# A delta rule and two expert layers on one core: one written order for all engines to the end of block 0, weights converted in pairs

## The chip, the core and the metric

One core of a Trainium2 chip runs one program. The metric is device time in microseconds, the median of repeated runs. The profile is one execution, taken by the hardware profiler.

## The reference, cut to what matters

```python
for t in range(S):                      # delta rule: B=4, H=8, S=768, D=48
    y[:, :, t] = einsum('bhd,bhde->bhe', q[:, :, t], state)
    v_old = einsum('bhde,bhd->bhe', state, k_n[:, :, t])
    state = state + beta_t * einsum('bhd,bhe->bhde', k_n[:, :, t], v[:, :, t] - v_old)
x = y as (3072, 384)
h = x @ w_in                            # layer 1: 384 -> 2048 -> 384
g = where(h >= 1, h, where(h <= -1, 0, (h + 1) ** 2 / 4));  x = g @ w_out
h = x @ w2_in;  r = maximum(h, 0);  out = (r * r) @ w2_out   # layer 2, same sizes
```

All inputs are float32; the kernel is handed the weights as the 64-bit words that the harness makes of them.

## The kernel before, in words

The sequence is cut into 24 chunks of 32 steps. For a chunk, small matmuls make the products of its keys (`gram`), a triangular matrix of 32 by 32 per batch and head is inverted (`tri`, for a group of up to four chunks at once, group sizes `GROUPS` = 2, 4, 4, ...), and then `chunk_steps` runs a chain: `ks` (state times keys, subtracted from the values on VectorE), `tr` (the inverse applied), `qs`/`pu` (the output), `ku` (the state's update), `xt` (transposition into `xh`, `xl`, the high and low parts that the expert layer multiplies). Chunks 0 and 1 (`HEADS`) have no state yet and use `cross_gram`.

The expert layers run in blocks of chunks (`SIZES` = 2, 2, 3, ...; block 0 is chunks 0 and 1, 256 columns). A block has 16 units f. Unit f multiplies `w_in` tile f (`hidden`: 9 matmuls into `h`), makes g on ScalarE and VectorE (L606 to L609), splits it into `gh` (ScalarE, L621) and `gl` (VectorE, L622), and two units later `out1` adds 9 matmuls into `acc`. Each block's third copy out of `acc`, like the converted tiles of layer 2, takes a buffer of the ring `wl`.

Each matmul operand is a high and a low part, so each weight tile must first be converted: ScalarE takes its two words apart (L178, L181, into tiles `wt` and `wl`), VectorE joins them (L187), ScalarE rounds to the high part (L198), VectorE subtracts for the low part (L202). A tile is 128x384; layer 1 has 32. `load_w` keeps at most two weight loads under way.

The order: to the end of the first inversion (on VectorE, in halves) everything stands as written. After that only TensorE's order is written (`manual_schedule(engines=ENGINES)`); a scheduler places the instructions of the other engines by its own estimates. The second group's inversion runs on GpSimd in 30 steps of a product (L423) and a sum (L424). Conversions are handed out by `more_w1`: 20 steps between the pieces of chunks 0 and 1, the rest in the slots of block 0 (two slots a unit). Block 0's slots from `HEAD` = 19 on also carry the steps of chunks 2 and 3, and slot 18 the transpose that ends the second inversion (`end1`, L427).

Of the kernel before, what the change touches and what calls it, by code (L numbers as in the profile page):

```python
# [25 lines left out]
def kernel(  # L26
# [39 lines left out]
    EAGER = 18  # L66
    AHEAD = 8
# [3 lines left out]
    WT, WL = 3, 4  # L71
    GB = 2
    MANY = 4
    HEAD = 19
# [14 lines left out]
    pairs = {}  # L89

    def weight(i, f):

        if (i, f) not in pairs:
            t = wp.tile([P, 2, DM], F32R, tag=f"w{i}{f}", name=f"w{i}{f}")
            pairs[i, f] = t[:, 0], t[:, 1]
        return pairs[i, f]
# [56 lines left out]

    def load_w(x, key):
        w, f, i = key
        pool, tag, bufs = ring, "raw", RAW
        if w == 0:
            pool, tag, bufs = wp, f"w{i}{f}", 1
        raw = raws[key] = pool.tile([P, DM, 2], I32, tag=tag, bufs=bufs, name="raw")
        ins = nc.sync.dma_start(  # L160
            raw.rearrange("p a b -> p (a b)"), (w1, w2)[w][f, i].bitcast(I32)
        ).ins
        if w == 0:
            sent.append(ins)
            if len(sent) > FLIGHT:
                tc.add_manual_dep(
                    ins, sent[-1 - FLIGHT].name,
                    mybir.DependencyInfo(mybir.DependencyClass.Sync, mybir.DependencyReason.DATA),
                    reason="at most FLIGHT weight loads under way",
                )  # L170


    def convert_stages(key, box):
        def s0():
            raw = raws.pop(key)
            t = box["w"] = tmp("wt", WT)
            b = box["t"] = tmp("wl", WL)
            nc.scalar.activation(  # L178
                t, raw[:, :, 1].bitcast(F32), AF.Prelu, scale=2.0 ** -112, alpha=2.0 ** 32
            )  # L180
            nc.scalar.activation(  # L181
                b.bitcast(I32), raw[:, :, 0].bitcast(U32), AF.Copy, scale=7.49 * 2.0 ** -32
            )

        def s1():
            t, bits = box["w"].bitcast(I32), box["t"].bitcast(I32)
            nc.vector.scalar_tensor_tensor(  # L187
                bits, t, 3, bits, ALU.logical_shift_left, ALU.bitwise_or
            )

        return [s0, s1]


    def part_stages(key, box):
        _, f, i = key

        def s3():
            nc.scalar.copy(weight(i, f)[0], box["t"])  # L198

        def s4():  # L200
            hi, lo = weight(i, f)
            nc.vector.tensor_sub(lo, box["t"], hi.bitcast(F32))  # L202

        return convert_stages(key, box) + [s3, s4]
# [3 lines left out]
    def weight_items(w):  # L208

        keys = [(w, f, i) for f in range(NF) for i in range(2)]  # L210
        if w == 0:
            keys.sort(key=lambda k: (k[1] + LAG * k[2], -k[2]))

        def item(x):
            _, f, i = keys[x]
            box = {}
            if w == 0:
                r = part_stages(keys[x], box)
            else:
                r = convert_stages(keys[x], box)  # L220
                r.append(lambda: nc.sync.dma_start(w2f[f, :, i], box["t"]))
            s1 = r[1]
            r[1] = lambda: (s1(), ahead(x + 1 + (RAW if w else AHEAD)))
            return r

# [3 lines left out]
        def ahead(end):  # L229
            while todo and todo[0][0] < end:  # L230
                load_w(*todo.pop(0))
# [34 lines left out]
    def value(c):  # L266

        g, j = group_of[c]
        nc.gpsimd.tensor_mul(
# [10 lines left out]
    def gram(c, lo=0, hi=2, late=0, eng=None, side=0):  # L280
# [43 lines left out]

    spare = {
        name: f"w{i}{NF - f}" for name, i, f in
        (("u0", 1, 1), ("u1", 1, 2), ("cross", 0, 1), ("z", 1, 3), ("l", 0, 2), ("d", 1, 4))
    }

    def cross_gram(a, c):  # L330
        x = cross[a, c] = wp.tile([P, H, 2, T], F32, tag=spare["cross"], name="cross")
# [14 lines left out]
    def tri(n, eng, halves=False):  # L346
        x = tx
        gm = ring.tile([P, T, T], F32, tag="gm", bufs=1, name="gm")
# [36 lines left out]
        def row():  # L385
            if halves:
                d = two(gm, both, both)
                eng.tensor_mul(
# [6 lines left out]
        def row2():  # L395
            if halves:
                eng.tensor_mul(
# [10 lines left out]
        def step(j):  # L408
# [15 lines left out]
            eng.tensor_add(rest, rest, t)  # L424
# [11 lines left out]
    def joined(n):  # L436
        l, z = (wp.tile([P, 2, H, T], F32, tag=spare[k], name=k) for k in "lz")
        d = wp.tile([P, GC * H, T2], F32, tag=spare["d"], name="d")
# [30 lines left out]
    def chunk_steps(c):  # L469
# [26 lines left out]
        def tr():  # L496
# [7 lines left out]
            else:  # L504
                us[c] = wp.tile([P, H, D], F32, tag=spare[f"u{c}"], name="u")
# [78 lines left out]
    def hidden(layer, n, f):  # L584
# [18 lines left out]
        if layer == 0:  # L603
# [3 lines left out]
            marks[1] = nc.vector.tensor_scalar(g, r, 2.0, 0.5, ALU.min, ALU.mult)  # L607
            nc.scalar.activation(g, g, AF.Square)  # L608
            nc.vector.scalar_tensor_tensor(g, r, -1.0, g, ALU.add, ALU.max)  # L609
        else:  # L610
# [3 lines left out]
        def rest():  # L614
# [6 lines left out]
            nc.scalar.copy(ghi, g)  # L621
            nc.vector.tensor_sub(glo, g, ghi.bitcast(F32))  # L622
            gs[layer, n, f] = (ghi, glo)
# [74 lines left out]
    def flow(items, lag=1):  # L698

        steps = []  # L700
        for x, it in enumerate(items):
            for i, st_ in enumerate(it):
                while len(steps) <= x * lag + i:
                    steps.append([])
                steps[x * lag + i].append(st_)
        return [lambda fs=fs: [f() for f in fs] for fs in steps]

# [7 lines left out]
    first1, w1s = weight_items(0)  # L715
    first2, w2s = weight_items(1)
    w1f = flow(w1s)
    w1f.reverse()

    SPREAD = 3  # L720
    behind = [nullcontext]

    def more_w1(m=1):
        with behind[0]():
            for _ in range(m):
                if w1f:
                    w1f.pop()()

    with tc.manual_schedule():
        for c in range(GROUPS[0]):  # L730
            load_kq(c)
        nc.sync.dma_start(bet, beta)
        for c in range(GROUPS[0], KQ):
# [3 lines left out]
        for c in range(HEADS):  # L737
            load_kv(c)
        first1(EAGER)
        nc.gpsimd.memset(zero, 0.0)  # L740
        nc.gpsimd.memset(one, 1.0)
        nc.gpsimd.memset(tiny, 1e-36)
        nc.scalar.activation(st[:, 0, 0, 0:1], one, AF.Sqrt, bias=zero)
        nc.gpsimd.memset(mask, 1.0)
        nc.gpsimd.memset(tx, 0.0)
        for b in range(B):
            for o, op in enumerate((ALU.is_ge, ALU.is_gt)):
                m_ = mask[T * b:T * (b + 1), o]
                nc.gpsimd.affine_select(
# [5 lines left out]
        for c in range(GROUPS[0]):  # L755
            gram(c, 0, 1)
        begin, pre, steps, end = tri(0, V, True)
        begin()
        go(pre)
        for c in range(HEADS):  # L760
            save0(c)
        go([gram(c, late=2, eng=G) for c in range(GFIRST[1], GFIRST[2])])
        cross_gram(0, 1)
        masks = [gram(c, 1, 2, late=2, eng=G) for c in range(HEADS)]
        go(steps)
        for c in range(HEADS):
            value(c)
        go(masks)
        end()
        rows0()  # L770
        begin, pre, steps, end1 = tri(1, G)
        begin()
        ins = go(pre[:-2])
        behind[0] = lambda: tc.issue_after(ins.ins)
    ENGINES = {mybir.EngineType.PE}
    with tc.manual_schedule(engines=ENGINES):
        for f in (ld0, dld0):
            for c in range(HEADS):
                f(c)
        go(pre[-2:])  # L780
        go(steps)
        chains = [chunk_steps(c) for c in range(HEADS)]
        (k0, t0, q0, p0, _, x0), (k1, t1_, q1, p1, _, x1) = chains
        for m, fs in enumerate([[k0, t0], [k1], [q0, p0], [t1_], [q1], [x0], [p1], [x1]]):
            go(fs)
            if m < 4:
                more_w1(5)
        behind[0] = lambda ins=marks[2]: tc.issue_after(ins.ins)
        turn[0] = None
        load_kv(HEADS)  # L790
        for c in range(KG):
            load_kg(KQ + KG + c)

        SL = 2 * NF
        exa, exb = {}, {}

        def put(n, slot, *fs):
            for i, f in enumerate(fs):
                exb.setdefault(SL * n + slot + i, []).append(f)

        def later(*fs):

            def one_(f):
                with tc.issue_after(marks[0].ins), tc.issue_after(marks[1].ins):
                    f()

            return [lambda f=f: one_(f) for f in fs]

        def put_a(n, slot, f):
            exa.setdefault(SL * n + slot, []).append(f)  # L810

        at, ready = {}, {}

        def two_grams(c):
            gram(c)
            gram(c + 1, side=1)

        after = {}
        for i, c in enumerate(range(GFIRST[2], GFIRST[3])):
            ready[c] = 4 + 3 * i
            put_a(0, ready[c], lambda c=c: gram(c))
        for g in range(3, NG):
            for i in range(GROUPS[g] // 2):
                after[GFIRST[g - 1] - 1 + i] = GFIRST[g] + 2 * i
        for n in range(1, NB):
            todo = []
            for c in range(FIRST[n], FIRST[n] + SIZES[n]):  # L830
                for i, s_ in enumerate(chunk_steps(c)):
                    todo.append(((at, c) if i == 0 else None, s_))
                if c in after:
                    x = after[c]
                    todo.append(((ready, x + 1), lambda x=x: two_grams(x)))
            for i, (mark, s_) in enumerate(todo):
                o = 0 if n > 1 else HEAD
                slot = SL * (n - 1) + o + i * (SL - o) // len(todo)
# [3 lines left out]
        put(0, HEAD - 1, *later(end1))  # L842
        for c in range(HEADS):
            put(0, 8 + 4 * c, lambda c=c: load_kq(c + KQ))
        for c in range(HEADS, NCH):
# [17 lines left out]
        for n in range(NB - 1):  # L863
            if n == 0:
# [95 lines left out]
```

## Time and profile before

| | us |
|---|---|
| median of 3 runs (1023.9 to 1025.18) | 1024.61 |
| the profiled execution | 1026.46 |
| its span, first to last instruction | 1024.7 |
| TensorE busy (95% of the span) | 968.4 |
| VectorE / ScalarE / GpSimd busy | 574.5 / 465.2 / 319.4 |

Engines are PE (TensorE), PEld (its weight loads), DVE (VectorE), ACT (ScalarE), POOL (GpSimd) and SP (which issues the DMAs). A row of a timeline names start, duration, engine, line, operation and tiles; in brackets stands how long the engine was idle before and what released it; "issue" means that it waited for nothing that the profile shows. A float32 matmul of the program shows as two rows' counts, a float32r one as one.

### The profile page before, as it was taken

To read this page: it belongs to the slowest core of one execution; us is meant where nothing else is said; L and a number is where in the kernel's file an instruction comes from. 1 tells how busy PE (TensorE), PEld (TensorE's weight loads), DVE (VectorE), ACT (ScalarE), POOL (GpSimd) and SP (SyncE) were. 2 spreads that over 40 slices of the span, in tenths; PEclk is the share of its full clock that TensorE was granted. 3 is DMA by queue.
4 is the path that set the end of the run, shared out by engine and by line. 5 is a ranking of instruction groups with operands and counts; after the bars stand their busy time and mean duration, and the time that the engine had idled before them with its cause. 6 is when DMAs were issued, how large, how long until landed. Compare 5 with 4: busy or idle time off the path is not lost.

```text
span 1024.7 us, 32087 instructions
## 1 busy us (share of the span) xinstructions
PE 968.4 (95%) x14152; PEld 902.6 (88%) x14152; DVE 574.5 (56%) x994; ACT 465.2 (45%) x935; POOL 319.4 (31%) x476
## 2 busy tenths in 40 slices
PE   5357899999999999999999999999999999999998
PEld 4347898999999999999999999989989999899997
DVE  6988565775666677677465676543343333333333
ACT  2776465554555545555445554333333333333332
POOL 3792780492077049368022121120020200200000
PEclk9999999999999999999999999999999999999999
DMA  9774154442532534312023223010010000000000
GB/s 265 222 215 142 49 152 133 129 142 61 174 101 80 157 88 133 111 39 96 3 71 90 67 79 95 6 55 8 1 62 1 1 32 1 31 1 1 31 1 31
DMA packets 35244, 80.83 MB, mean 79 GB/s; under 512 B 4512, under 2 KB 15264, under 8 KB 35104
## 3 DMA queue, kind: packets, MB, share of 16 engines
q1 hardware_dynamic: 35104, 78.78, 25.9%
q8 instruction: 111, 1.82, 0.8%
q14 instruction: 29, 0.24, 0.1%
HBM read 63.03 MB, written 15.73 MB: 77 GB/s over the span
## 4 chain that ended last, share of the span: by engine, by line
PE 87%; DMA 6%; DVE 3%; ACT 2%; issue 1%; SPq 0%; ACTq 0%; DVEq 0%
PE acc L574 39%; PE h L574 38%; DMA raw<-in_w_dram 5%; PE yy L518 2%; PE sps L530 2%; PE tr L498 2%; PE ks L484 2%; PE g L293 1%; PE yy L484 1%; PE xt L559 1%; DMA kqt<-in_kq_dram 1%; DVE wl L187 0%; DVE g L609 0%; DVE w L202 0%; DVE gp L427 0%
## 5 line engine op out<-in xcount | busy, mean ns | idle before, releaser
L574 PE MATMUL acc<-w,gg 128*128 128x384 f32 x1152 | 218.4, 337 | 2.1 <-ACT e L629 2.1
L574 PEld LDWEIGHTS acc<-w,gg 128*128 128x128 f32 x1152 | 204.5, 187 | 10.7 <-ACT e L629 3.0
L574 PE MATMUL h<-x2s,w 128*128 128x512 f32 x864 | 213.8, 392 | 0.0
L574 PEld LDWEIGHTS h<-x2s,w 128*128 128x128 f32 x864 | 160.9, 188 | 28.3
L574 PE MATMUL h<-xh,w 128*128 128x384 f32 (+1 forms) x864 | 164.6, 327 | 3.5 <-ACT r L606 2.8
L574 PE MATMUL acc<-gh,w 128*128 128x384 f32 (+1 forms) x864 | 163.7, 325 | 1.6 <-ACT gh L621 1.6
L612 DVE TENSOR_TENSOR rg<-rg 128x512 f32<-128x512 f32 x96 | 71.3, 743 | 141.4 <-ACT rg L611 141.4
L574 PEld LDWEIGHTS h<-xh,w 128*128 128x128 f32 x864 | 139.6, 193 | 6.7 <-ACT r L606 3.7
L574 PEld LDWEIGHTS acc<-gh,w 128*128 128x128 f32 x864 | 136.7, 189 | 5.2 <-ACT gh L621 1.7
L611 ACT ACTIVATE rg<-h,zero 128x512 f32<-128x512 f32 x96 | 66.0, 687 | 137.4 <-PE h L574 137.4
L622 DVE TENSOR_TENSOR gg<-rg,gg 128x512 fp32r<-128x512 f32 x96 | 66.7, 695 | 104.5 <-ACT gg L621 104.5
L622 DVE TENSOR_TENSOR gl<-g,gh 128x384 fp32r<-128x384 f32 (+1 forms) x144 | 88.0, 611 | 64.5 <-ACT gh L621 60.3
L423 POOL TENSOR_TENSOR t<-tx,gm 128x30 f32<-128x30 f32 (+9 forms) x180 | 110.0, 611 | 19.3 <-DVE tx L402 5.9
L621 ACT CAST gh<-g 128x384 fp32r<-128x384 f32 (+1 forms) x144 | 68.7, 477 | 102.7 <-DVE g L609 78.4
L606 ACT ACTIVATE r<-h,one 128x384 f32<-128x384 f32 (+1 forms) x144 | 78.3, 543 | 81.5 <-PE h L574 80.3
L424 POOL TENSOR_TENSOR tx<-tx,t 128x30 f32<-128x30 f32 (+9 forms) x180 | 110.6, 615 | 14.0
L621 ACT CAST gg<-rg 128x512 fp32r<-128x512 f32 x96 | 59.7, 622 | 119.7 <-PE acc L574 112.7
L609 DVE SCALAR_TENSOR_TENSOR g<-r,g 128x384 f32<-128x384 f32 (+1 forms) x144 | 88.5, 614 | 39.9 <-ACT g L608 37.4
L607 DVE TENSOR_SCALAR g<-r 128x384 f32<-128x384 f32 (+1 forms) x144 | 62.4, 434 | 68.1 <-ACT r L606 67.1
L608 ACT ACTIVATE g<-g 128x384 f32<-128x384 f32 (+1 forms) x144 | 70.2, 487 | 54.5 <-DVE g L607 53.7
L574 PE MATMUL acc<-gl,w 128*128 128x384 f32 (+1 forms) x432 | 90.8, 318 | 1.9 <-DVE gl L622 1.9
L574 PE MATMUL h<-xl,w 128*128 128x384 f32 (+1 forms) x432 | 91.8, 322 | 0.0
(99 smaller groups left out, 923.9 us busy)
## 6 DMA issues: line engine op xcount, KB each, us to landing
raw<-in_w_dram SPq DMA_DIRECT2D x64, 384.0 KB, 3.8
kqt<-in_kq_dram SPq DMA_DIRECT2D x88, 192.0 KB, 4.1
kv<-in_kv_dram SPq DMA_DIRECT2D x24, 384.0 KB, 3.6
w2f<-wl SPq DMA_DIRECT2D x32, 192.0 KB, 3.1
w2r<-w2f SPq DMA_DIRECT2D x16, 384.0 KB, 3.0
x2r<-x SPq DMA_DIRECT2D x6, 768.0 KB, 4.8
out_dram<-e SPq DMA_DIRECT2D x23, 192.0 KB, 2.0
x<-e SPq DMA_DIRECT2D x18, 192.0 KB, 2.1
```

Of the source, the lines that this page charges most:

```text
L423: eng.tensor_mul(t, by.to_broadcast(shape), of.to_broadcast(shape))
L424: eng.tensor_add(rest, rest, t)
L484: per_bh(lambda b, h, p, pd: nc.tensor.matmul(o[p, h], kqt[c][pd, b // 2, h, x * T:(x + 1) * T], st[pd, b // 2, h], start=h == 0, stop=x = ...
L574: nc.tensor.matmul(o, *((r, l) if swap else (l, r)), **flags)
L606: marks[0] = nc.scalar.activation(r, h, AF.Relu, bias=one)
L607: marks[1] = nc.vector.tensor_scalar(g, r, 2.0, 0.5, ALU.min, ALU.mult)
L608: nc.scalar.activation(g, g, AF.Square)
L609: nc.vector.scalar_tensor_tensor(g, r, -1.0, g, ALU.add, ALU.max)
L611: marks[0] = nc.scalar.activation(r, h, AF.Relu, bias=zero)
L612: marks[1] = nc.vector.tensor_mul(g, r, r)
L621: nc.scalar.copy(ghi, g)
L622: nc.vector.tensor_sub(glo, g, ghi.bitcast(F32))
```

## The change

Weights of layer 1 are loaded into tiles of two (`weights`), taken apart in place, joined, rounded and subtracted 768 wide; the layout of the spare rooms follows (`room`). `tri` gains an argument that no call uses. Both halves of the products of chunks 0 and 1 come from one set of matmuls (`gram_of_head`). The `wl` ring has three buffers instead of four, `wt` is gone. The first three loads of layer 2 move behind block 0, and the last six of layer 1 behind unit 3. Up to the end of block 0 the order of all engines is written; inside a unit the conversions stand at four fixed places (`between`). After it only TensorE's order is written, as before.

```diff
-    WT, WL = 3, 4
+    WL = 3
...
+    def sign_bits(raw):
+        low, high = raw[..., 0], raw[..., 1].bitcast(F32)
+        return (
+            lambda: nc.scalar.activation(high, high, AF.Prelu, scale=2.0 ** -112, alpha=2.0 ** 32),
+            lambda: nc.scalar.activation(
+                low, low.bitcast(U32), AF.Copy, scale=7.49 * 2.0 ** -32),
+        )
...
+    def upper(x):
+        nc.scalar.copy(weights(x)[:, :, 0], words[x])
+
+    def lower(x):
+        t = weights(x)
+        nc.vector.tensor_sub(t[:, :, 1], words.pop(x), t[:, :, 0].bitcast(F32))
...
+    EARLY, READY, HELD = 6, 3, 6
...
+        def part(x):
+            if x == 0:
+                if a is not None:
+                    make(a)
+                some(1)
+            elif x == 1:
+                if a is not None:
+                    upper(a)
+            elif x == 2:
+                some(1)
+            elif a is not None:
+                lower(a)
...
+        ins = go(steps)
+        rows0()
+        end()
+        after(value(0), ins)
+        value(1)
...
+        begin1()
+        s0()
+        t0()
+        pre1[0]()
+        whole_bits(2)
+        s1()
+        t1_()
+        go(pre1[1:])
+        steps1[0]()
+        value(2)
+        go(steps1[1:])
...
+        put_a(0, 4, k0)
+        put(0, 20, end1)
...
+        for c, at_ in ((2, (21, 22, 24, 26)), (3, (26, 27, 29, 31))):
...
-            a = max(a, HEAD) if g == 2 else a
+            a = max(a, 22)
...
+        for x in range(NF):
+            unit(x, between(x))
+    with tc.manual_schedule(engines={mybir.EngineType.PE}):
+        for x in range(NF, total):
+            unit(x)
```

ScalarE, from the copy of chunk 1's `u` (after `tr`) to its `xh`. Before:

```order
L506 COPY u<-tr 128x384
L181 ACTIVATE wl<-raw 128x384 x2
L198 CAST w_1084<-wl 128x384
L178 ACTIVATE wt<-raw 128x384
L181 ACTIVATE wl<-raw 128x384
L561 CAST xh<-xt 128x3x128
L198 CAST w_1094<-wl 128x384
L178 ACTIVATE wt<-raw 128x384
L198 CAST w_1212<-wl 128x384
L178 ACTIVATE wt<-raw 128x384
L181 ACTIVATE wl<-raw 128x384
L523 COPY kv<-yy 128x384
```

Changed (L549 is now the copy of `u`, L566 that of the output, L180 and L181 take a pair apart, L217 rounds it):

```order
L549 COPY room<-tr 128x384
L217 CAST w_852<-wl 128x2x384
L180 ACTIVATE raw<-raw 128x768
L181 ACTIVATE raw<-raw 128x768
L566 COPY kv<-yy 128x384 x2
L604 CAST xh<-xt 128x3x128
L217 CAST w_967<-wl 128x2x384
L604 CAST xh<-xt 128x3x128
```

Between the copy of `u` and that of the output stood ten conversion instructions before; now three, of two pairs.

VectorE around the transpose that ends the second inversion and the first subtraction of chunk 2's chain. Before (L427, L494):

```order
L393 TENSOR_TENSOR gm<-gm,st_1935 128x512
L607 TENSOR_SCALAR g<-r 128x256
L427 STREAM_TRANSPOSE gp<-tx 128x32x32
L622 TENSOR_TENSOR gl<-g,gh 128x256
L609 SCALAR_TENSOR_TENSOR g<-r,g 128x256
L494 TENSOR_TENSOR kv<-kv,ks 128x384
```

Changed (L468, L537), with a whole unit ahead of it: L650 and L653 make g, L187 joins a pair, L668 is `gl`, L221 subtracts the pair:

```order
L650 TENSOR_SCALAR g<-r 128x256
L187 SCALAR_TENSOR_TENSOR wl<-raw 128x768
L653 SCALAR_TENSOR_TENSOR g<-r,g 128x256
L668 TENSOR_TENSOR gl<-g,gh 128x256
L221 TENSOR_TENSOR w_1577<-wl,w_1577 128x2x384
L468 STREAM_TRANSPOSE gp<-tx 128x32x32
L537 TENSOR_TENSOR kv<-kv,ks 128x384
```

The conversions now stand in front of this transpose and in the two units behind it; before, none was left there.

## Rows read from the trace of the kernel before

**Rows 1.** The profile's page: its span, and TensorE's busy tenths in 40 slices.

```profile
span 1024.7 us, 32087 instructions
...
PE   5357899999999999999999999999999999999998
```

**Rows 2.** Uses of tile raw to 110 us: ScalarE idle before it, us and times.

```profile
  DMA raw<-in_w_dram: 14.8, 8
```

**Rows 3.** Timeline of PE to 68 us: start, duration, engine, line, operation [idle before <-releaser].

```profile
28.30 1.54 PE L293 MATMUL g<-kqt 48*32 48x32 f32 x97 [2.67 <-issue]
...
43.26 1.00 PE L498 MATMUL tr<-kv,gp 32*32 32x48 f32 x34 [2.92 <-issue]
...
60.51 1.50 PE L518 MATMUL yy<-u,gp 32*32 32x48 f32 x64 [4.48 <-ACT u L506]
...
66.12 0.90 PE L559 MATMUL xt<-ident,kv 128*128 128x128 f32 x3 [4.11 <-ACT kv L523]
...
67.59 1.65 PE L574 MATMUL h<-xh,w 128*128 128x256 f32 x6 [0.57 <-ACT xh L561]
```

**Rows 4.** Timeline of ACT: chunk 1's last copy, and prices by width.

```profile
65.61 0.46 ACT L523 COPY kv<-yy 128x384 f32<-128x384 f32 x1
...
90.20 0.54 ACT L178 ACTIVATE wt<-raw 128x384 f32<-128x384 f32 x1
...
91.08 0.45 ACT L606 ACTIVATE r<-h,one 128x256 f32<-128x256 f32 x1
```

**Rows 5.** Timeline of DVE in the first inversion.

```profile
12.31 1.20 DVE L379 TENSOR_TENSOR st<-st 128x32 f32<-128x32 f32 x1
...
21.66 1.33 DVE L423 TENSOR_TENSOR t<-tx,gm 128x72 f32<-128x72 f32 x1
...
23.02 1.20 DVE L424 TENSOR_TENSOR tx<-tx,t 128x72 f32<-128x72 f32 x1
...
25.30 2.06 DVE L427 STREAM_TRANSPOSE gp<-tx 128x1024 f32<-128x1024 f32 x1
```

**Rows 6.** Timeline of POOL: a mask product, and three steps of the second inversion.

```profile
12.19 1.26 POOL L309 TENSOR_TENSOR gp<-gp,mask 128x512 f32<-128x512 f32 x1 [7.06 <-ACT gp L306]
...
37.13 0.48 POOL L423 TENSOR_TENSOR t<-tx,gm 128x30 f32<-128x30 f32 x1 [1.57 <-DVE tx L402]
...
55.76 0.83 POOL L424 TENSOR_TENSOR tx<-tx,t 128x234 f32<-128x234 f32 x1
...
82.17 0.27 POOL L424 TENSOR_TENSOR tx<-tx,t 128x30 f32<-128x30 f32 x1
```

**Rows 7.** Timeline of DVE: three widths alone, and one beside a GpSimd step.

```profile
36.97 0.55 DVE L202 TENSOR_TENSOR w<-wl,w 128x384 fp32r<-128x384 f32 x1
...
56.02 0.99 DVE L187 SCALAR_TENSOR_TENSOR wl<-wt,wl 128x384 int32<-128x384 int32 x1
...
88.48 0.43 DVE L609 SCALAR_TENSOR_TENSOR g<-r,g 128x256 f32<-128x256 f32 x1
...
89.78 0.68 DVE L309 TENSOR_TENSOR gp<-g,mask 128x512 f32<-128x512 f32 x1
```

**Rows 8.** Timeline of PE from unit 10 of block 0 to the first unit of block 1.

```profile
106.88 0.97 PE L574 MATMUL h<-xh,w 128*128 128x256 f32 x6
...
109.59 0.88 PE L498 MATMUL tr<-kv,gp 32*32 32x48 f32 x64 [1.39 <-DVE kv L494]
...
121.26 0.28 PE L484 MATMUL yy<-st,kqt 48*32 48x48 f32 x7 [1.81 <-issue]
...
121.47 1.62 PE L574 MATMUL h<-xh,w 128*128 128x256 f32 x6
...
132.66 0.84 PE L574 MATMUL h<-xh,w 128*128 128x256 f32 x6
```

**Rows 9.** Timeline of DVE: the transpose that ends the second inversion.

```profile
106.33 2.13 DVE L427 STREAM_TRANSPOSE gp<-tx 128x1024 f32<-128x1024 f32 x1
```

**Rows 10.** DMA issues: operation, count, KB each, median us to landing.

```profile
w2f<-wl SPq DMA_DIRECT2D x32, 192.0 KB, 3.1
```

More of the change, by code (lines that the diff above doesn't have):

```diff
@@ L88, with weights @@
     st = cst.tile([P, B2, H, D], F32, name="st")
-    pairs = {}
+    needed = [(0, f, i) for f in range(NF) for i in range(2)]
+    needed.sort(key=lambda k: (k[1] + LAG * k[2], -k[2]))
+    place_of = {k[2:0:-1]: divmod(x, 2) for x, k in enumerate(needed)}
+    both = {}
+    def weights(x):
+        if x not in both:
+            both[x] = wp.tile([P, 2, 2, DM], F32R, tag=f"w{x}", name=f"w{x}")
+        return both[x]
     def weight(i, f):
[L93 to L96, printed above, removed]
+        x, m = place_of[i, f]
+        return weights(x)[:, m, 0], weights(x)[:, m, 1]
     s_ps = [ps.tile([P, H, D], F32, name=f"sps{i}") for i in range(B2)]
@@ L696, in split_x2 @@
         return [s0, s1]
[L698 to L706, printed above, removed]
     def go(fs):
@@ L714 @@
     V, G = nc.vector, nc.gpsimd
[L715 to L718, printed above, removed]
+    first2, w2s = weight_items()
+    SL = 2 * NF
     SPREAD = 3
[L721 to L727, printed above, removed]
+    NW, NP = 2 * NF, NF
+    EARLY, READY, HELD = 6, 3, 6
+    exa, exb = {}, {}
+    bits = [f for x in range(EARLY, NP) for f in (lambda x=x: halves(x)[0](), lambda x=x: halves(x)[1]())]
@@ new lines, with some, between @@
+    bits.reverse()
+    def some(m):
+        for _ in range(m):
+            if bits:
+                bits.pop()()
+    def between(f):
+        a = READY + f if READY + f < NP else None
+        def part(x):
[10 more added lines that the diff above has]
+                lower(a)
+        return part
@@ new lines, in put, with later, one_, put_a @@
+    def put(n, slot, *fs):
+        for i, f in enumerate(fs):
+            exb.setdefault(SL * n + slot + i, []).append(f)
+    def later(*fs):
+        def one_(f):
+            with tc.issue_after(marks[0].ins), tc.issue_after(marks[1].ins):
+                f()
+        return [lambda f=f: one_(f) for f in fs]
+    def put_a(n, slot, *fs):
+        exa.setdefault(SL * n + slot, []).extend(fs)
+    def two_grams(c):
+        gram(c)
+        gram(c + 1, side=1)
+    def run(ex, x):
+        for f in ex.pop(x, ()):
+            f()
@@ new lines, with out_, unit, after @@
+    blocks = [(0, n) for n in range(NB)] + [(1, n) for n in range(NM)]
+    total = NF * len(blocks)
+    def out_(x):
+        g, f = divmod(x, NF)
+        (out1, out2)[blocks[g][0]](blocks[g][1], f)
+    def unit(x, between=lambda x: None):
+        g, f = divmod(x, NF)
+        rest = hidden(*blocks[g], f, between)
+        run(exa, 2 * x)
+        rest()
+        run(exb, 2 * x)
+        if x >= LAG:
+            out_(x - LAG)
+        run(exa, 2 * x + 1)
+        run(exb, 2 * x + 1)
+    def after(ins, first):
+        tc.add_manual_dep(
+            ins.ins, first.ins.name,
+            mybir.DependencyInfo(mybir.DependencyClass.Sync, mybir.DependencyReason.DATA),
+            reason="GpSimd keeps still beside the inversion",
+        )
@@ L763 @@
-        cross_gram(0, 1)
-        masks = [gram(c, 1, 2, late=2, eng=G) for c in range(HEADS)]
-        go(steps)
+        masks += [gram(c, late=2, eng=G) for c in range(KQ, KQ + KG)]
+        whole_bits(0)
+        ins = go(steps)
[3 more added lines that the diff above has]
+        value(1)
         for c in range(HEADS):
-            value(c)
+            mask_of_head(c)
         go(masks)
[L769 to L772, printed above, removed]
@@ new lines @@
+        go(steps1[1:])
+        upper(1)
+        lower(1)
+        whole_bits(3)
+        make(2)
+        q1()
+        q0()
+        p0()
+        p1()
+        x0()
+        upper(2)
+        x1()
+        lower(2)
+        whole_bits(4)
+        whole_bits(5)
+        turn[0] = None
+        put_a(0, 4, k0)
+        put(0, 20, end1)
+        put_a(0, 6, k1)
+        put(0, 7, lambda: [load_w(needed[x]) for x in range(NW - HELD, NW)])
+        for c in range(HEADS):
+            put(0, 8 + c, lambda c=c: load_kq(c + KQ))
@@ new lines, with steps_of @@
+        put(0, 21, lambda: value(3))
+        for c, at_ in ((2, (21, 22, 24, 26)), (3, (26, 27, 29, 31))):
+            def steps_of(c=c, box={}):
+                if c not in box:
+                    box[c] = chunk_steps(c)
+                return box[c]
+            for i, slot in enumerate(at_):
+                put_a(0, slot, lambda i=i, g=steps_of: g()[i]())
+        put(0, SL - 1, lambda: first2(RAW))
+        at, ready = {}, {}
+        for c, slot in zip(range(GFIRST[2], GFIRST[3]), (9, 12, 15, 18)):
+            ready[c] = slot
@@ L841 @@
                 put_a(0, slot, s_)
[L842 to L845, printed above, removed]
+        for c in range(4, NCH):
             put(0, max(0, at[c] - 5), lambda c=c: value(c))
```

259 lines of the change are left out of this document (121 added, 138 removed).

## The prediction, as it was put on record

> **What bounds the kernel now.** I read the page first: TensorE's busy tenths are 5, 3, 5, 7 and 8 in the first five slices, 128 us, and 9 in all others but the last [rows 1]. From block 1 on it has next to nothing to wait for, so the change, which alters the order up to block 0's end, can be worth no more than what TensorE loses before that. I measure it by one mark: the start of block 1's first matmul of an expert layer, 132.66 us [rows 8]. What comes behind that mark is the same TensorE work in both kernels; a shift of the mark is a shift of the end, apart from two small terms at the end of this sum.
>
> Then I read the timeline of TensorE up to the first expert matmul, at 67.59 us [rows 3]. Two sorts of idle time stand there. One is called "issue": between 28.30 and 43.26 us TensorE stops every 128 rows' counts, four stops with three pitches of (43.26 - 28.30) / 3 = 5.0 us, although the matmuls in between take only about 1.5 us of each and nothing that the profile shows is missing. So the stretch is paced by the number of matmuls, not by their work; I take it for the loading of TensorE's code, since the stops come by count. The other sort is a wait for ScalarE: 4.48 us for the copy of `u` and 4.11 us for the copy of chunk 1's output. That copy takes 0.46 us [rows 4]; it is late because ScalarE's queue is in front of it full of weight conversions, which sit 14.8 us in all, 8 times, waiting for loads [rows 2].
>
> **The change part by part.**
>
> *The way to the first expert matmul.* The products of chunks 0 and 1 are made once instead of in two goes: 64 float32 matmuls fewer ahead of the chain, which is 128 counts, one pitch: -5.0 us. On ScalarE three conversion instructions instead of ten stand between chunk 1's copy of `u` and that of its output, and they belong to pairs 1 and 3, whose loads no longer queue behind three loads of layer 2; so the waits of 4.48 and 4.11 go: -8.6 us. GpSimd's mask products no longer stand in the first inversion: three VectorE instructions that took 1.20, 1.33 and 1.20 us there, for 32 or 72 elements [rows 5], shrink to about 0.2 each, 3.1 us in all, and the inverse's first half is transposed ahead of the other transpose of 2.06 us. Most of this 5.2 us is covered by the code stops, which pace TensorE at the same time; I take 1 us. Sum -14.6: the first expert matmul at 67.6 - 14.6 = 53.0 us. Bounds: 55 if the inversion's gain counts for nothing and one stop moves onto the chain, 49 if all of it counts.
>
> *The pace of block 0's first ten units.* This is new, since now every unit carries a pair. No 768-wide pass is in the trace. On VectorE 256, 384 and 512 elements take 0.43, 0.55 and 0.68 us [rows 7], some 0.125 per 128, so 768 take 0.68 + 0.25 = 0.93; not below 0.8, and not above two narrow ones, 1.10. On ScalarE 256 and 384 take 0.45 and 0.54 [rows 4], so 768 take about 0.81, at most 1.08. I take the values by slope, since overhead is paid once. A unit on VectorE is three 256-wide instructions at 0.43 and two wide ones at 0.93, 3.15 us; on ScalarE two wide passes and a rounding at about 0.81 and three instructions of up to 0.45, 3.8 us. The chain from `r` through g, `gh` and `gl` crosses both queues, so a unit without other disturbance takes about 4 us.
>
> GpSimd disturbs it. A 384-wide join that takes 0.55 alone takes 0.99 beside the second inversion's steps, while such a step takes 0.83 [rows 7, 6]: each VectorE instruction waits 0.44. Five of them: 3.15 + 2.2 = 5.35 us a unit. The inversion takes 45.3 us, from 37.13 to 82.44 [rows 6]; now its inputs are ready at about 43 us, so it ends at about 88 to 92.
>
> The Trainium skill (SBUF — State Buffer, Who interferes with whom) says that two-input VectorE instructions and GpSimd share one port pair by an exclusive lock, and whoever comes second is blocked for the other's whole instruction. The first inversion's rows agree: 1.20 us for 32 elements beside a mask product of 1.26 [rows 5, 6]; the join at 0.99 does not show a whole wait, as 0.44 is about half a step. By the rule taken whole the sum would be 12 us higher, as the first rival has it.
>
> The first three units go into three PSUM tiles without waiting for g; with 1.65 us for six of a unit's nine matmuls [rows 3] they and the state's update take some 7 us, so unit 3 starts at 60. Six units at 5.35 bring unit 9 to 92, when the inversion has ended, and unit 9 takes 4: unit 10 at 96 us, against 106.88 now [rows 8]. Of the 14.6 us 10.9 are left, because conversions that were spread over the waits for weights now stand in the units.
>
> *The tail of block 0.* From unit 10 to block 1 it takes 132.66 - 106.88 = 25.8 us now. Three things are added. VectorE's subtraction for chunk 2 now has a pair's low part directly in front of it and the transpose of 2.13 us [rows 9] behind a full unit; TensorE's wait for it, 1.39 us now [rows 8], grows by about 3 (0.9 to 4). Units 10 to 12 carry the last three pairs, 6 x 0.93 = 5.6 us of VectorE; half of it lies in time that VectorE spends waiting for `gh`: +2.8 (0 to 5.6). The third group's transpose and norms move from ahead of unit 10 into units 11 and 12: +1.6 (0 to 2.1). The tail takes 25.8 + 7.4 = 33.2 us: block 1 at 129.2, 3.5 us earlier.
>
> *Behind block 0.* With three `wl` buffers instead of four, the third copy out of `acc` can wait for a store of 3.1 us [rows 10] in each of the five blocks that convert layer 2, and TensorE for it one unit later; a unit of lead hides nearly all of it: +0.3 (0 to 3). The third inversion starts later by two or three slots with the same due slot: +0.2 (0 to 2.2). Moved loads of layer 2 cost nothing: they are not read before block 1; without that cover each is one load.
>
> **The sum.** -3.5 + 0.5 = -3.0 us: the profiled execution's 1026.46 becomes 1023.5. It stands 1.85 above the median of the runs, so the median of 1024.61 becomes **1021.6**.
>
> **The rivals.**
>
> *The inversion becomes the bound (slower).* Two wide instructions a unit hold VectorE's side almost twice as long as narrow ones, and a GpSimd step waits as well. If each of the 60 steps gets its turn only once per VectorE instruction, five per unit of 5.35 us, they take 60 x 1.07 = 64 us and end at 107. `end1`'s transpose stands in VectorE's queue at about 101; everything that VectorE has for units 10 and 11 stands behind it. From an end later than 101 on it decides; at 107 it costs 6 us: 1027.6. If besides each VectorE instruction waits out a whole step of 0.83, a unit takes 3.15 + 4.15 = 7.3 us, six of them 12 more than in the sum, and the end comes at 1033; of this rival's 0.20 I give that 0.05, since the one wait in the rows is half a step. This is what the rule of the Trainium skill (SBUF — State Buffer, Who interferes with whom) would do here. Against the whole rival: VectorE has gaps in each unit in which steps follow each other freely.
>
> *The early start is kept.* If the tail's three additions lie in idle time, the mark comes 10.9 us earlier: 1013.7. For it speaks that VectorE and ScalarE have gaps in the tail now; against it that the chain of chunks 2 and 3 there passes through VectorE's queue in order.
>
> *The change does not do what it says, net.* The tail gives the whole lead back, since it also has a code stop: the one at 121.26 us cost 1.81, and the six matmuls behind it took 1.62 us where 0.97 is usual [rows 8]. A written order cannot step around a late instruction. If such a stop falls on another chain matmul, or a second one comes, 3 to 4 us go: 1024.6.
>
> **How the numbers follow.** What a measurement of this kernel can tell from no change is about 0.2%, 2 us. My sum gets 0.42, the inversion as bound 0.20, the kept start 0.20, nothing net 0.18. Of my sum's own spread (1018 to 1025 by the bounds) three quarters lie below 1022.5: faster 0.31 + 0.20 = 0.51; no change 0.08 + 0.11 = 0.19; slower 0.03 + 0.07 + 0.20 = 0.30. The range takes in the kept start almost wholly and the inversion's rival with some of its spread, 1014.5 to 1029.0; the likeliest case alone has 1018 to 1025.
>
> **What would show it.** In the new profile: the first expert matmul at 50 to 55 us, without waits for ScalarE of over 4 us ahead of it; units 3 to 9 at 5 to 5.5 us; wide VectorE passes of 0.9 us alone and up to 1.4 beside GpSimd; the second inversion's last step before 100 us; unit 10 near 96; block 1 near 129. I am wrong in the first step if the first expert matmul starts after 60, in the second if units run faster than 4.5 us beside GpSimd, in the third if the tail takes under 28 or over 36 us, and the last terms are wrong if the end moves by over 2 us more or less than the mark.

## The result and the profile after

The changed kernel takes 1037.77 us (median of 5 runs, 1033.66 to 1038.17), the kernel before 1023.90 beside it: 1.0124 times as long by the means (1036.74 and 1024.01), 95% interval [1.0102, 1.0146]. I had predicted 1021.6, between 1014.5 and 1029.0. The profiled execution has a span of 1036.3 us, 11.6 more than before.

The page of the changed kernel: span, TensorE's busy tenths and its granted clock in 40 slices.

```profile
span 1036.3 us, 31739 instructions
...
PE   5665889999999999999999999999999999999998
...
PEclk9988889999999999999999999999999999999999
```

TensorE is busier than before in the second and third slice and less so in the fourth and the sixth [rows 1], and its clock is lower from the third to the sixth. Starts of the expert matmuls `h` by unit, from TensorE's timeline, in us, show where the time went:

| unit | before | changed | difference |
|---|---|---|---|
| 0 | 67.59 | 44.38 | -23.2 |
| 3 | 81.83 | 51.73 | -30.1 |
| 7 | 98.26 | 75.78 | -22.5 |
| 8 | 100.49 | 86.35 | -14.1 |
| 10 | 106.88 | 93.26 | -13.6 |
| 14 | 126.14 | 122.64 | -3.5 |
| 16 (block 1) | 132.66 | 131.25 | -1.4 |
| 18 | 139.52 | 138.66 | -0.9 |
| 21 | 149.51 | 154.62 | +5.1 |
| 27 | 170.93 | 179.10 | +8.2 |
| 35 | 200.22 | 209.74 | +9.5 |

A lead of 30 us is lost in pieces, and the loss goes on behind block 1's start. TensorE's timeline of the changed kernel (start, duration, instruction, in brackets the idle time before it and its releaser):

```profile
44.38 0.98 PE L617 MATMUL h<-xh,w 128*128 128x256 f32 x6 [1.06 <-ACT xh L604]
...
83.80 0.39 PE L304 MATMUL g<-kqt 48*32 48x64 f32 x2 [5.63 <-DMA kqt<-in_kq_dram]
...
103.29 1.50 PE L541 MATMUL tr<-kv,gp 32*32 32x48 f32 x64 [4.70 <-DVE kv L537]
104.72 1.65 PE L617 MATMUL acc<-gh,w 128*128 128x256 f32 x6
...
117.56 1.51 PE L527 MATMUL yy<-st,kqt 48*32 48x48 f32 x64 [3.23 <-DVE xl L605]
...
131.25 0.97 PE L617 MATMUL h<-xh,w 128*128 128x256 f32 x6 [1.54 <-ACT xh L604]
...
145.21 0.80 PE L617 MATMUL acc<-gh,w 128*128 128x256 f32 x2 [2.99 <-DVE e L676]
...
146.45 1.48 PE L617 MATMUL h<-xh,w 128*128 128x256 f32 x6
...
150.92 0.87 PE L617 MATMUL h<-xh,w 128*128 128x256 f32 x6
...
163.38 0.27 PE L561 MATMUL yy<-kv,gp 32*32 32x48 f32 x3 [1.66 <-issue]
```

The long waits are paid twice. Six matmuls that take 0.87 us at 2.4 GHz take 1.48 to 1.65 just behind the waits of 4.70 and 2.99 us; in the window from 140 to 150 us the granted clock is 0.70 of full speed, and 1.00 in the one before it. Behind the wait of 1.54 us at 131.25 they take 0.97. The stop at 163.38, with the lower clock behind it, makes 1.9 of the 3.1 us that are lost from unit 21 to 27; the kernel before has a stop of 1.29 us at 157.91, with a granted clock of 1.00 around it.

The wait at 145.21 is new. VectorE's timeline at that place, then ScalarE's:

```profile
140.62 0.43 DVE L650 TENSOR_SCALAR g<-r 128x256 f32<-128x256 f32 x1 [0.22 <-ACT r L649]
144.73 0.42 DVE L676 COPY e<-acc 128x256 f32<-128x256 f32 x1 [3.69 <-DMA w2f<-wl]
```

```profile
146.59 0.41 ACT L666 CAST gh<-g 128x256 fp32r<-128x256 f32 x1 [4.07 <-DVE g L653]
```

All three copies out of `acc` at a block's end take `wl` buffers. The third needs the one that holds a converted tile of layer 2 until its store has landed. VectorE stands still for 3.69 us, and with it the next unit's g and the rounding on ScalarE. At 208.78 us TensorE waits 1.49 us in the same way; behind block 1's start there are four such waits, 5.0 us in all.

The wait at 83.80 is SP's (first row of a run of transfers, time to the end of the run, count):

```profile
66.05 11.17 SPq L165 DMA_DIRECT2D raw<-in_w_dram  x6
77.27 21.92 SPq L136 DMA_DIRECT2D kqt<-in_kq_dram  x14
```

The last six weight loads, put into slot 7, go out two at a time until 77 us; chunk 8's load of slot 9 stands behind them, and TensorE's next instruction is that chunk's product.

### The profile page after: what moved, and what is told of

The parts are those of the page before. It is cut to its first block, busy times and chain, and to the rows that moved or that the text cites. A ratio compares the mean times of both kernels' runs of the same rounds, so it can differ in the third digit from the quotient of the medians.

```text
span 1036.3 us, 31739 instructions
## 1 busy us (share of the span) xinstructions
PE 977.3 (94%) x14024; PEld 908.8 (88%) x14024; DVE 570.4 (55%) x962; ACT 461.2 (45%) x887; POOL 323.4 (31%) x476
## 4 chain that ended last, share of the span: by engine, by line
PE 85%; DVE 6%; DMA 4%; ACT 3%; issue 2%; SPq 0%; ACTq 0%; DVEq 0%
PE acc L617 38%; PE h L617 37%; PE tr L541 2%; PE yy L561 2%; PE g L304 2%; PE sps L573 1%; DMA w2f<-wl 1%; PE ks L527 1%; PE yy L527 1%; DMA kqt<-in_kq_dram 1%; DVE wl L187 1%; PE xt L602 1%; DVE gl L668 1%; ACT w L217 1%; DVE w L221 1%
## 5 line engine op out<-in xcount | busy, mean ns | idle before, releaser
L617 PEld LDWEIGHTS acc<-w,gg 128*128 128x128 f32 x1152 | 204.4, 187 | 10.8 <-ACT e L676 3.2
L617 PE MATMUL acc<-gh,w 128*128 128x384 f32 (+1 forms) x864 | 168.5, 331 | 8.3 <-DVE e L676 5.0
L617 PEld LDWEIGHTS acc<-gh,w 128*128 128x128 f32 x864 | 139.9, 194 | 13.5 <-DVE e L676 6.2
L668 DVE TENSOR_TENSOR gl<-g,gh 128x384 fp32r<-128x384 f32 (+1 forms) x144 | 89.8, 624 | 72.9 <-ACT gh L666 64.0
L668 DVE TENSOR_TENSOR gg<-rg,gg 128x512 fp32r<-128x512 f32 x96 | 66.8, 695 | 104.0 <-ACT gg L666 104.0
L465 POOL TENSOR_TENSOR tx<-tx,t 128x30 f32<-128x30 f32 (+9 forms) x180 | 113.9, 633 | 14.0
L653 DVE SCALAR_TENSOR_TENSOR g<-r,g 128x384 f32<-128x384 f32 (+1 forms) x144 | 94.4, 655 | 39.7 <-ACT g L652 37.5
L650 DVE TENSOR_SCALAR g<-r 128x384 f32<-128x384 f32 (+1 forms) x144 | 63.5, 441 | 63.4 <-ACT r L649 62.9
```

Source lines behind the costliest of these rows:

```text
L465: return eng.tensor_add(rest, rest, t)
L617: nc.tensor.matmul(o, *((r, l) if swap else (l, r)), **flags)
```

## The experiments

All medians and ratios are against runs of the kernel before on the same chip. First the four suspects: the ring, the queue, the third group's norms in the tail, and all together.

**Own buffer.**
```diff
-                evac(m, o, x2[...], "wl", WL)
+                evac(m, o, x2[...], *(("we", 1) if m == KT - 1 else ("wl", WL)))
```


> The third copy out of acc at a block's end gets a buffer of its own instead of the next of the three wl buffers. Theory (ring): in the changed kernel that copy stands at the head of VectorE's queue 3.7 us long behind a store of layer 2's converted words, TensorE waits 2.99 us at 145.2 and 1.49 us at 208.8 for it, and its clock falls after the first; all of that goes, 5 to 8 us: 1030 to 1033 us. Rival (late anyway): VectorE would be late at the block's end without the ring, so the wait only changes its name: 1036 to 1038 us.


Measured: 1028.54, ratio 1.0049 [1.0027, 1.0071]. The wait for `e` is gone; from unit 18 to 21 it takes 11.7 us instead of 16.0. With the own buffer there are four again. The ring it was, and its price is about 7.7 us (1.0124 - 1.0049 of 1024), some 3 us either way by the two intervals. Where it is paid, the first matmul of layer 2 shows, in the kernel before, the changed one and this one:
```profile
614.27 2.21 PE L574 MATMUL h<-x2s,w 128*128 128x512 f32 x9
...
625.97 2.21 PE L617 MATMUL h<-x2s,w 128*128 128x512 f32 x9
...
614.06 2.21 PE L617 MATMUL h<-x2s,w 128*128 128x512 f32 x9
```
From block 1's start to there the kernel before takes 481.6 us, the changed one 13.1 more, this one 2.3 more. Block 1 itself starts at 130.13 here instead of 131.25, though this edit changes no step up to there: a mark can differ by about 1 us without a cause in the edit.

**Load ahead.** Slots of the third group's products:
```diff
-(9, 12, 15, 18)
+(6, 12, 15, 18)
```


> The product of chunk 6 moves from slot 9 to slot 6, so that chunk 8's load stands on SP's queue ahead of the six last weight loads. Theory (queue): the wait of 5.63 us at 83.8 us goes; unit 8 starts at 80 to 82 instead of 86.35, and block 1 starts 3 to 6 us earlier: 1032 to 1035 us. Rival (the tail takes it): the second inversion still ends at about 92 and the tail waits for its transpose, so block 1 starts at most 1.5 us earlier: 1036 to 1038 us.


Measured: 1031.45, ratio 1.0077 [1.0050, 1.0105]. Unit 8 starts at 79.76, as the theory says; but the wait went to the next chunk, whose load is still behind the six:
```profile
89.54 0.39 PE L304 MATMUL g<-kqt 48*32 48x64 f32 x2 [4.10 <-DMA kqt<-in_kq_dram]
```
Block 1 starts at 131.06, only 0.2 us earlier, as the rival has it. Behind it the ring's wait is 1.93 us here instead of 2.99; why that moved, and the rest of the 6 us between the medians, these traces do not say. The traced execution took 1036.33, the slowest of the seven (from 1027.95).

**Third group later.**
```diff
-            a = max(a, 22)
+            a = max(a, 28)
```


> The third group's transpose and norms start at slot 29 instead of 23, behind the steps of chunk 2 and most of those of chunk 3. Theory (the tail is a chain through VectorE's queue): the transpose of 2.11 us and the norms of about 1.4 us leave the chain of chunk 2; the waits at 113 to 118 us shrink by 3 us and the slow matmuls behind them go: block 1 starts 3 to 5 us earlier, 1032 to 1035 us. Rival (they lay in idle time, and the third inversion becomes late): block 1 less than 1 us earlier, and block 2 waits for the third inversion, 1037 to 1042 us.


Measured: 1039.90, ratio 1.0150 [1.0123, 1.0177]. Theory and rival are each right in part: block 1 starts at 128.35, 2.9 us earlier, and block 2 pays 7.08 us, since VectorE's queue stands for 6.50 at the transpose that waits for the third inversion's last sum on GpSimd:
```profile
173.16 2.07 DVE L468 STREAM_TRANSPOSE gp<-tx 128x1024 f32<-128x1024 f32 x1 [6.50 <-POOL tx L465]
...
176.50 1.50 PE L527 MATMUL ks<-st,kqt 48*32 48x48 f32 x64 [7.08 <-DVE gp L320]
```

**All three.**


> The three edits together. Theory (four separate waits, each with its price): block 1 starts at 121 to 126 us instead of 131.25 and nothing is lost behind it: 1018 to 1026 us. Rival (one bound behind all, VectorE's conversions): the edits don't add up, 1030 to 1035 us.


Measured: 1036.04, ratio 1.0123 [1.0098, 1.0147]. That is outside both forecasts. Block 1 starts at 124.92, 6.3 us earlier, then block 2 waits 9.77 us for the third inversion, more than that lead. So the sum of the other two was still open.

**Loads in pairs**, with the own buffer:
```diff
-        put(0, 7, lambda: [load_w(needed[x]) for x in range(NW - HELD, NW)])
+        for i in range(3):
+            put(0, 7 + 3 * i, lambda i=i: [load_w(needed[NW - HELD + 2 * i + m]) for m in range(2)])
...
-            put(0, 8 + c, lambda c=c: load_kq(c + KQ))
+            put(0, 16 + c, lambda c=c: load_kq(c + KQ))
```


> Own buffer as in the first experiment, and the six last weight loads go out as three pairs at slots 7, 10 and 13 (and the two loads of key and query chunks at 16 and 17), so that both chunk loads of the third group stand ahead of weight loads. Theory (separate waits): no wait for a chunk's load is left; unit 10 starts at 88 to 90 us instead of 93.26, block 1 at 124 to 127: 1018 to 1024 us, no slower than before. Rival (the tail is bound by the second inversion, which ends at about 92, and by VectorE): unit 12 still starts after 105 and block 1 after 129, and the time is that of the first experiment, 1027 to 1030 us.


Measured: 1025.31, ratio 0.9992 [0.9974, 1.0009]. No wait for a load is left, unit 10 starts at 89.93. The two mends bring back the whole 1.2%, though the block 1 mark moves by only 1.4 us against the run with the own buffer. It starts at 128.77, behind the theory's 124 to 127: the tail still takes 38.8 us, and its first wait grew from 4.70 to 5.28:
```profile
100.68 1.50 PE L541 MATMUL tr<-kv,gp 32*32 32x48 f32 x64 [5.28 <-DVE kv L537]
```

**Three tries at the tail** by moving steps in VectorE's queue: third group from slot 20 (`a = max(a, 19)`), the second inversion's transpose at slot 18 with chunks 2 and 3 two slots earlier, and both, each on top of loads in pairs.


> As the run of loads in pairs, and the third group's transpose and norms start at slot 20 instead of 23. Theory (the tail is one chain through VectorE's queue): they now stand directly ahead of chunk 2's subtraction and hold it by up to 3 us, but leave the chain of units 11 to 13: block 1 within 2 us of the run of loads in pairs, the end too, since the third inversion was not late there. Rival (the third inversion is late already in the changed kernel): block 2 gains 2 to 4 us.

> As the run of loads in pairs, and the transpose behind the second inversion moves from slot 20 to 18, the steps of chunks 2 and 3 by two slots. Theory (place in the queue): the inversion ends by 93 us, so the transpose costs VectorE at most 3 us of waiting and chunk 2's chain starts a unit earlier: block 1 2 to 4 us earlier than in the run of loads in pairs. Rival (the inversion is the bound there): VectorE stands at the transpose for over 4 us, units 9 and 10 become late by as much, and block 1 starts no earlier.

> The two last edits together (third group from slot 20, the second inversion's transpose at 18). Theory (place in the queue): as the better of the two alone or 1 to 3 us better, 1014 to 1021 us. Rival (VectorE's queue is full there): the two get in each other's way and the time is that of the worse of them or above.


Measured: 1.0044 [1.0025, 1.0062], 1.0035 [1.0020, 1.0051] and 1.0029 [1.0007, 1.0052]: all worse than loads in pairs. In the first the third group's transpose stands, with the second's, directly ahead of chunk 2's subtraction, and the wait for that is 7.10 us. In the second VectorE does not wait for the inversion (its last step starts at 92.91, the transpose at 95.02), block 1 starts 1.6 us earlier, and block 2 waits 3.72 us for the third inversion. The two together wait 7.34 us for `xl` at 119. What is moved forward there puts something else behind.

**Work between.**
```diff
-((2, (21, 22, 24, 26)), (3, (26, 27, 29, 31)))
+((2, (20, 23, 24, 26)), (3, (27, 28, 30, 31)))
```


> As the run of loads in pairs, with chunk 2's steps at slots 20, 23, 24, 26 instead of 21, 22, 24, 26 and chunk 3's at 27, 28, 30, 31 instead of 26, 27, 29, 31: its subtraction now stands ahead of the second inversion's transpose in VectorE's queue, and TensorE has the expert matmuls of a unit between a chunk's step and the next that waits for it. Theory (TensorE's own order makes it wait, with work right behind): the waits of 5.28 us for chunk 2's subtraction and 3.23 us for xl shrink by 1.5 to 3 us each, with the slow matmuls behind them; block 1 at 122 to 126 us instead of 128.8, the end at 1018 to 1022 us. Rival (VectorE's queue is full there): the waits move behind, block 1 at 128 or later, 1024 to 1027 us.


Measured: 1025.68, ratio 0.9998 [0.9981, 1.0015]. The waits shrink to 2.72 and 2.17 us, a new one of 1.87 appears, and block 1 starts at 127.35, 5.3 us ahead of the kernel before. At unit 28 2.8 us of it are left (171.58 against 174.41), at the span's end 0.2. The time is the rival's.

**Low parts on GpSimd**, on top of it (`eng = nc.gpsimd if x >= 13 else nc.vector` in `lower`).


> As the run with work between, and the low parts of the last three pairs (units 10 to 12) are computed on GpSimd, which is idle there, instead of VectorE. Theory (VectorE's queue is the chain of the tail): 3 x 0.95 us leave it, block 1 another 1 to 3 us earlier. Rival (port, latency): a 768-wide pass takes over 1.5 us on GpSimd and holds VectorE's passes meanwhile, block 1 no earlier or up to 2 us later.


Measured: 1.0005 [0.9989, 1.0021], block 1 at 127.99: the rival. GpSimd's pass and VectorE's next one, `gl`, twice (the lines are one further down in this kernel):
```profile
97.76 1.86 POOL L222 TENSOR_TENSOR w<-wl,w 128x768 fp32r<-128x768 f32 x1 [2.82 <-ACT w L217]
98.02 1.88 DVE L669 TENSOR_TENSOR gl<-g,gh 128x256 fp32r<-128x256 f32 x1 [0.41 <-ACT gh L667]
...
103.80 1.82 POOL L222 TENSOR_TENSOR w<-wl,w 128x768 fp32r<-128x768 f32 x1 [3.21 <-ACT w L217]
104.06 1.85 DVE L669 TENSOR_TENSOR gl<-g,gh 128x256 fp32r<-128x256 f32 x1 [0.87 <-ACT gh L667]
```
`gl` takes 1.88, 1.85 and, at the third, 1.10 us, where it takes 0.43 each time with work between. VectorE is spared 3 x 0.95 us and loses 3.5. Whether the three passes were on the chain this run therefore does not tell.

**Narrow passes**: the changed kernel, each 768-wide pass as two.


> The changed kernel with every 768-wide pass of a pair's conversion as two 384-wide ones, nothing else. Theory (cost by pass): VectorE 2 x 0.55 instead of 0.95 us and one more wait for GpSimd's step per split pass: 0.3 to 1.2 us more in each unit from 3 to 9, block 1 later by 2 to 7 us, 1040 to 1046 us. Rival (wide passes hold GpSimd and the other work up): units no slower, 1034 to 1038 us.


Measured: 1038.74, ratio 1.0119 [1.0104, 1.0134]. Block 1 starts at 135.68, 4.4 us later, as the theory says, but the end is that of the changed kernel within what can be told, below the theory's 1040 to 1046: the wide passes are worth 4.4 us up to block 1, and nothing that shows at the end.

**Four loads under way** (`FLIGHT = 4`), nothing else.


> The changed kernel with four weight loads under way at a time instead of two. Theory (TensorE's code comes through the same DMA engines, and in the changed kernel it comes faster since less else is moved): the stops up to 35 us lengthen by 1 us or more each and the first expert matmul starts at 47 to 52 us instead of 44.38. Rival (the stops don't depend on other transfers): first expert matmul at 44 to 45 us.


Measured: 1038.74, ratio 1.0118 [1.0102, 1.0133]. TensorE's timeline:
```profile
20.74 2.87 PE L304 MATMUL g<-kqt 48*32 48x64 f32 x97 [2.84 <-issue]
...
30.99 1.51 PE L500 MATMUL w<-gp,room 32*32 32x16 f32 x98 [4.00 <-issue]
...
52.77 1.65 PE L617 MATMUL h<-xh,w 128*128 128x256 f32 x6 [1.03 <-ACT xh L604]
```
In the changed kernel the stops at these places are 1.45 and 1.53 us:
```profile
20.46 2.87 PE L304 MATMUL g<-kqt 48*32 48x64 f32 x97 [1.45 <-issue]
...
28.37 1.56 PE L500 MATMUL w<-gp,room 32*32 32x16 f32 x99 [1.53 <-issue]
```
So the stops depend on what else the DMA engines move, and the first expert matmul comes 8.4 us later. Unit 7 still comes 8.4 us later (84.17 against 75.78), unit 8 and block 1 only 2.3 and 2.4 us, and the median is the same. That does not make the early start worthless: the edit also lets the six loads of slot 7 go out four at a time, all out by 69.03 us instead of 77.22, and the wait for chunk 8's load is gone.
```profile
62.69 6.34 SPq L165 DMA_DIRECT2D raw<-in_w_dram  x6
```
What a late start alone would cost, this run does not show.

**Few steps**: work between, with 28 of the second inversion's 30 steps left out (`go(steps1[1:3])`).


> As the run with work between, but 28 of the 30 steps of the second group's inversion are left out, so GpSimd does next to nothing beside units 0 to 9 and the values of chunks 2 to 5 are not those of the reference. Theory (GpSimd's steps hold VectorE's passes up): a 768-wide join takes 0.95 us, a low part 0.95 instead of 1.3, a unit from 4 to 9 takes 4.0 to 4.3 us instead of 4.9, unit 10 starts at 86 to 88 us instead of 91.2 and block 1 3 to 5 us earlier. Rival (VectorE's and ScalarE's own passes set the pace): a unit still takes 4.7 us or more, unit 10 starts after 90.


Measured: 1019.22, ratio 0.9931 [0.9906, 0.9955]. VectorE's groups from 52 to 92 us (count, busy us, mean ns, idle before), first with work between, then with few steps:
```profile
L221 DVE TENSOR_TENSOR w<-wl,w 128x768 fp32r<-128x768 f32 x9 | 12.0, 1330 | 0.0
L187 DVE SCALAR_TENSOR_TENSOR wl<-raw 128x768 int32<-128x768 int32 x9 | 8.9, 994 | 0.0
L653 DVE SCALAR_TENSOR_TENSOR g<-r,g 128x256 f32<-128x256 f32 x8 | 6.5, 815 | 0.0
L650 DVE TENSOR_SCALAR g<-r 128x256 f32<-128x256 f32 x9 | 5.4, 595 | 0.0
L668 DVE TENSOR_TENSOR gl<-g,gh 128x256 fp32r<-128x256 f32 x9 | 5.1, 570 | 4.1 <-ACT gh L666 4.1
```
```profile
L221 DVE TENSOR_TENSOR w<-wl,w 128x768 fp32r<-128x768 f32 x10 | 9.5, 952 | 0.0
L187 DVE SCALAR_TENSOR_TENSOR wl<-raw 128x768 int32<-128x768 int32 x10 | 9.5, 951 | 0.0
L668 DVE TENSOR_TENSOR gl<-g,gh 128x256 fp32r<-128x256 f32 x10 | 4.3, 426 | 6.9 <-ACT gh L666 6.9
L653 DVE SCALAR_TENSOR_TENSOR g<-r,g 128x256 f32<-128x256 f32 x10 | 4.2, 422 | 0.3 <-ACT g L652 0.2
L650 DVE TENSOR_SCALAR g<-r 128x256 f32<-128x256 f32 x10 | 3.5, 351 | 1.6 <-ACT r L649 1.6
```
The five passes of a unit take 3.10 us alone and 4.30 beside GpSimd. Units 4 to 10 come every 4.0 us ((87.09 - 60.55 - 2.58 for a load) / 6) instead of every 4.9 ((91.17 - 61.96) / 6), and block 1 starts 4.4 us earlier. GpSimd's steps hold the units up, as the theory says, by 0.9 us of 4.9. What is left is about ScalarE's own work; its groups in the same 40 us with few steps:
```profile
L181 ACT ACTIVATE raw<-raw 128x768 int32<-128x768 uint32 x10 | 9.2, 919 | 0.0
L217 ACT CAST w<-wl 128x768 fp32r<-128x768 f32 x10 | 8.3, 834 | 2.0 <-DVE wl L187 1.7
L180 ACT ACTIVATE raw<-raw 128x768 f32<-128x768 f32 x9 | 8.3, 920 | 0.2
L649 ACT ACTIVATE r<-h,one 128x256 f32<-128x256 f32 x10 | 4.6, 462 | 2.2 <-PE h L617 2.2
L652 ACT ACTIVATE g<-g 128x256 f32<-128x256 f32 x10 | 4.1, 412 | 0.8 <-DVE g L650 0.8
L666 ACT CAST gh<-g 128x256 fp32r<-128x256 f32 x10 | 4.0, 402 | 0.0
```
The six take 3.95 us a unit, nearly the whole 4.0, and VectorE waits 6.9 us for `gh`.

**Units free**: loads in pairs, with only TensorE's order given from unit 0 on.


> As the run of loads in pairs, but from the first expert matmul on only TensorE's order is given; the order of the other engines is left to the scheduler already in block 0, as in the kernel before. Theory (VectorE's work up to block 1 is the bound, whatever its order): block 1 within 2 us of 128.8. Rival (the given order is what makes chunk 2's subtraction and xl late): the waits in the tail go, block 1 more than 3 us earlier. Other rival (without the order the conversions crowd ahead of the units' short passes): units 3 to 6 start over 8 us later, block 1 over 3 us later.


Measured: 1054.57, ratio 1.0269 [1.0226, 1.0313]. The first expert matmul itself comes at 78.07, block 1 at 154.30: the other rival, and earlier than it said, since conversions already crowd ahead of the chain of chunks 0 and 1, for whose copies TensorE waits:
```profile
62.12 1.50 PE L561 MATMUL yy<-room,gp 32*32 32x48 f32 x64 [5.58 <-ACT room L549]
70.35 0.90 PE L602 MATMUL xt<-ident,kv 128*128 128x128 f32 x3 [6.74 <-ACT kv L566]
```
Without the given order the early start is lost altogether. But the first rival is half right too: the last conversion of layer 1 on VectorE ends at 117.1 us here, and the tail behind it, from unit 10 (129.12) to block 1, takes 25.2 us without a wait above 1.3. Whether the order or the conversions in the tail make it long elsewhere, this run does not separate.

## Why the prediction was wrong

**The way to the first expert matmul** was right in kind and too small: 44.38 us instead of 53.0 (bounds 49 to 55). The waits of 4.48 and 4.11 us went. The mis-sized term is the pitch of the stops, 5.0 us: I carried it over from before, as if it belonged to the number of matmuls alone. The stops up to the first expert matmul take 17.8 us in all before and 6.3 in the changed kernel, where the last three are 0.38, 1.53 and 1.00 us; with four loads under way they grow again.

**The pace of block 0** held between the waits: units 4 to 7 come every 4.94 us ((75.78 - 60.97) / 3; 5.35 predicted), the inversion's last step starts at 91.58 (88 to 92 predicted), unit 10 at 93.26 (96). The wide pass alone takes 0.95 us (0.93). The wait for GpSimd was over-sized: 1.2 us a unit by the run with few steps, not 5 x 0.44. ScalarE's 3.95 us a unit were foreseen (3.8). Two waits are in no step of the prediction: 4.53 us for ScalarE's `r` ahead of unit 4, which makes 9.2 us from unit 3 to 4, and the 5.63 us at 83.8. I wrote that moved loads of layer 2 "cost nothing" and never asked what stands behind the moved loads of layer 1 on SP.

**The rule taken whole** (the Trainium skill, SBUF — State Buffer, Who interferes with whom) fell as the rival used it, with a whole step of wait in each of the five passes: beside GpSimd's steps, which take 0.87 and 0.94 us in the mean from 52 to 92 us with work between, the joins lose 0.04 us each and the other four passes 0.14 to 0.39. In a single meeting the trace agrees with the rule: with the low parts on GpSimd, `gl`, which starts 0.26 us behind GpSimd's pass of 1.86, takes 1.88 us. What the rival had wrong is that every pass comes second.

**The tail** took 38.0 us (131.25 - 93.26) instead of 33.2, outside 28 to 36. The wait for chunk 2's subtraction grew by 3.3 us, as priced (3). Not priced were the wait of 3.23 us for `xl` and the lower clock behind both. How the 38.0 us divide between the conversions, the transposes and the order there, no run separates. So the mark is at 131.25, 1.4 us earlier instead of 3.5.

**Behind block 0** is the step that failed most: +0.5 us predicted, at most 5.2 by the bounds; in the spans 11.6 + 1.4 = 13.0 us. "A unit of lead hides nearly all of it" treated the copy as TensorE's business alone. The copy stands in VectorE's queue, which runs in order: the next unit's g waits with it, ScalarE's rounding behind that, and TensorE's clock falls. The run with the own buffer shows the ring's price, about 7.7 us by the runs and 10.8 in the traces. Without it the kernel is still 0.49% slower than before, and that goes with the wait for chunk 8's load, as the run with loads in pairs shows: the pace of block 0 is the second step that failed. How those 5.8 us (1.0049 - 0.9992) reach the end stays open, since block 1's start moves by 1.4 us only and the spans by 2.4 (1025.1 and 1022.7).

**The rivals.** The inversion did not become the bound through its end: its transpose starts at 100.77, 9 us after the last step. The early start was not kept. That the tail gives back all was nearest for the mark, but not for the end. None of the three had the ring, which I had listed as a term with a bound of 3 us.

**Open:** with both mends and work between, block 1 starts 5.3 us earlier, and the time does not change within 0.2%. TensorE gives 2.5 us back by unit 28, with stops of 0.52 and 1.65 us and the lower clock behind them, and 1.9 us between 885 and 912 us, in layer 2. There it waits a little longer for a copy than the kernel before, whose row comes second:
```profile
892.80 1.32 PE L617 MATMUL acc<-w,gg 128*128 128x384 f32 x6 [1.93 <-ACT e L676]
...
894.46 1.32 PE L574 MATMUL acc<-w,gg 128*128 128x384 f32 x6 [1.69 <-ACT e L629]
```
The granted clock is 0.83 from 890 to 900 us, in the kernel before 1.00 from 892 to 902. Whether that is more than chance was not tried. A lead is not always lost behind block 1: with few steps block 1 starts 4.4 us earlier than with work between, and the span is 5.6 us shorter (1018.9 and 1024.5). No version with all its steps that beats the kernel before was found.

## What to carry to other kernels

Before a ring is made smaller, look at which in-order queue the waiting instruction stands in, and count what is behind it there, not only who reads its result. When a batch of transfers is moved, list every later transfer on the same queue and its reader; split the batch rather than hold the reader. An earlier start is worth only what the waits behind it leave: follow the lead unit by unit, and name the wait that takes each piece. When an experiment delays the start on purpose, see first that it moves no later wait as well.

## What the runs showed that I had not expected

TensorE's stops every 128 counts depend on other transfers: with four weight loads under way the load queue takes 97.7% of the DMA engines between 10 and 45 us, and two stops take 2.84 and 4.00 us; with two it takes 79.2%, and the same stops take 1.45 and 1.53. In the kernel before it takes 91.0%, with stops of 2.55 to 3.85 us.

GpSimd's steps hold VectorE's passes unevenly: a join of 0.95 us loses 0.04, the 256-wide pass L653 nearly doubles, from 0.42 to 0.82 us. The step can be the one held: at 48.34 us in the changed kernel a sum of 150 elements that starts 0.01 us behind a join takes 1.27 us, and 0.49 at 86.27.
